# Layer norm of the first tiles in fewer VectorE steps, the transposes of the gradient half ahead of those of the next filter, and an empty slot more

## The chip, the cores and the metric

The kernel runs on one NeuronCore of a Trainium2 chip. The metric is the device time of one execution in microseconds (us), as a median over several executions. The profile is of one further execution.

The engines are named as the profile names them: PE is TensorE (matmuls; PEld its weight loads), DVE is VectorE, ACT is ScalarE, POOL is GpSimd, and SP is the queue that issues most DMAs. L938 means line 938 of the kernel before.

## The reference

Forward and backward pass of a layer that adds two branches to its input. Cut to what matters:

```python
xn = layernorm(q)                                  # [2048, 1024], eps 1e-5, steps rounded to bf16
# branch A: long convolution over the sequence, by FFT in the reference
kv  = shift(k, shift_k) * v                        # 4 taps
y   = irfft(rfft(kv) * rfft(ssm_k)) + kv * ssm_D   # one filter per channel
A   = xn * y
# branch B: gated MLP, 1024 -> 3584 -> 1024
gate, up = xn @ W_gate, xn @ W_up
h = relu(gate) * up
out = q + A + h @ W_down
# and, for a given grad_out, the gradients of q, k, v, shift_k, ssm_k, ssm_D, W_gate, W_up, W_down
```

Inputs and outputs are bf16, sums in PSUM are f32.

## The kernel before

The program is one stream for each engine. Branch B's matmuls are the bulk of the work. Branch A's are threaded between them.

**Phases of branch B.** `hidden` makes the layer norm and, in 14 blocks (seven column blocks of 512 for each half of the 16 row tiles), the matmuls of the gate (`ps_g`), of up (`ps_u`) and of the hidden gradient (`ps_h`), eight matmuls of 128x512 to a group. `grad_down` (`ps_d`) and `grad_in` (`ps_w`) make the weight gradients. `out_phase` (`ps_o`) and `grad_x` (`ps_x`) make the output and the input's gradient; nothing of branch A runs beside these two.

**The head.** The 16 row tiles are normed in chunks: four single tiles, then pairs (`LN_CHUNKS`). `layer_norm` is a generator; each `next` runs it to its next `yield`. For a chunk it does:

- the row sums on ScalarE (L866), for tile 0 with half of the columns on VectorE (L877);
- the mean in bf16 (L882 or L884), a cast of it to f32 (L891) and the subtraction (L895), all on VectorE;
- the squares, again on ScalarE (L866), with half of the columns on VectorE (L870) for tiles 0 and 1;
- the variance (L882 or L884), plus epsilon (L906), and the square root on ScalarE (L907);
- a Newton step for the root: reciprocal (L909), two products and sums (L912, L913), the reciprocal of the result (L914);
- the scaling (L920) and the store of the normed tile (L921, POOL's queue).

`flip_xn` then transposes the tile on the PE (L970, `pst_x`) and copies it to SBUF (L973). The gate of that tile waits for the copy. `first_gate_up` runs gate and up of tiles 0 to 3, with the transposes of the next tile in the middle of an up group. Before all of this `warm(17)` issues 17 dummy matmuls (L985), which depend on nothing but a memset. VectorE also makes relu(gate) * up for each up group: L1044 takes `ps_u` out of PSUM, L1046 makes `ht`. For each gradient group ScalarE copies `ps_h` (L1144) and VectorE multiplies (L1145).

**Order on the engines.** Most instructions carry a priority, and a scheduler orders those of an engine by it. `keep_in_program_order` and `pin` fix single instructions where the program issues them. Every engine then runs its own stream strictly in order: an instruction that waits holds everything queued behind it.

**Branch A.** `steps` and `slots` write it as a list of slots. Each slot holds at most one PE part and one VectorE part. It handles eight groups of 128 channels one after another. `first` begins the first group; `slots` does the rest of a group and the beginning of the next. Every slot has a nominal length (`SLOT` 1900 ns; in the dense phases `DENSE`, 1900 or 1250 ns), and every group of branch B's matmuls has one too. A slot is emitted when the nominal lengths of branch B have caught up with those of the slots so far. So a slot more moves all that follows by about one group of eight matmuls of branch B.

The transforms are matmuls with small tables (line 72: `FW`, `R`, `IA`, `RB`). Their PSUM tiles, two buffers, are copied by ScalarE (L76). Between two stages VectorE transposes 32x32 blocks (L327, two instructions of 128x1024 for a transpose, in `flip`). Of these the change touches:

- `flip_H`: the spectrum of the next group's filter, from `Bh` (after `add_D`, two small additions); read by `fwd2` about 60 us later;
- `flip_C(self.Cg, 0)`, called `flg`: the gradient half, from `Cg`, which `inv_a` and ScalarE write; read by `inv_b`, whose result `gkv` gives `gks`, which `tap_sums` (`ps<-kp,gks`) reads;
- `flip_B(self.Bk, 1)`, called `flK`: the last of a group's beginning; read by `fwd2_pair`.

**Queues.** SP issues the loads and most stores in program order: rows of x (`ln_x`), weight blocks (`wg`, `wu`, and `wdT` and `goT` by DMA transposes), and branch A's loads and stores. In the last block of `grad_down`, the normed rows come back as `xn_nat` (L961), and between them lie branch A's stores of y (`y_d`) and of the filter's gradient (`ghn`). When branch A is done, `open_right` loads `W_down` (`wd`, L1360) for `out_phase`.

Of the kernel before, what the change touches and what calls it, by code (L numbers as in the profile page):

```python
# [14 lines left out]
ALU = mybir.AluOpType  # L15
ACT = mybir.ActivationFunctionType
# [32 lines left out]
class ABranch:  # L49
# [36 lines left out]
    def load(self, out, in_):  # L86
        self.pri.now()
        ins = self.nc.sync.dma_start(out=out, in_=in_)
        if self.pin:
            self.tc.keep_in_program_order(ins)  # L90
        else:
            self.pri.pin(ins)
# [533 lines left out]
    def slots(self, st, gi):  # L626
        G, K, H, GKV = self.G, self.K, self.H, self.GKV
        if gi == 0:
            yield from self.first(st)
        nx, n2 = self.ahead(st, 1), self.ahead(st, 2)  # L630
        last = nx is None
        f2 = self.fwd2_pair()
        yield f2, None
        yield None, None
        yield f2, None
        yield None, None
        yield f2, None
        yield None, lambda: self.turn(G, 0, -1, slice(0, 4))
        q = self.cmul(H, G, True, GKV, 0)
        yield f2, q  # L640
        yield None, q
        yield None, q
        yield None, q
        yield None, q
        yield None, lambda: self.turn(G, 0, -1, slice(4, 8))
        iaG = self.inv_a()
        q = self.cmul(H, G, True, GKV, 1)
        yield None, q
        yield iaG, q
        yield None, q  # L650
        f1h = None
        if not last:
            self.need(self.load_filter, nx)
            self.need(self.load_rest, nx)
            f1h = self.fwd1_filter(nx)
        yield f1h, q
        yield None, q
        yield f1h, lambda: self.turn(H, 1, 1)
        self.fetch(n2, self.load_filter)
        q = self.cmul(K, G, True, G, 0)  # L660
        yield None, q
        yield iaG, q
        yield None, q
        if not last:
            self.need(self.load_g, nx)
            flH = self.flip_H()
            yield None, self.both(lambda: self.add_D(nx), flH)
            yield None, flH
        flg = self.flip_C(self.Cg, 0)
        yield None, flg  # L670
        yield None, flg
        yield None, q
        yield None, q
        q = self.cmul(H, K, False, K, 0)
        yield self.inv_b(st, "gkv", 0), q
        yield None, q
        yield None, q
        gkv = st["gkv"]
        gks = st["gks"] = self.ttile("gks")
        yield None, lambda: self.tt(gks[:, 0:16, :], gkv[:, 0:16, :], st["vt"][:], ALU.mult)  # L680
        self.fetch(nx, self.load_v)
        gv = self.ttile("gv")
        yield None, lambda: self.tt(gv[:, 0:16, :], gkv[:, 0:16, :], st["ksh"][:], ALU.mult)
        self.store_time(self.out_gv, st["cg"], gv)
        yield None, q
        yield None, self.both(lambda: self.halo(st), q)
        yield lambda: self.tap_sums(st), None
        self.fetch(nx, self.load_k, self.load_taps)
        f1g = None
        if not last:  # L690
            self.need(self.load_xn, nx)
            yield None, lambda: self.gate_grad(nx)
            self.fetch(n2, self.load_xn)
            f1g = self.fwd1(self.Bg, nx["gt"])
        yield None, lambda: self.tap_diagonals(st)
        ia = self.inv_a_pair()
        q = self.cmul(K, G, True, G, 1)
        yield ia, q
        yield None, q
        yield ia, q  # L700
        yield None, q
        yield None, q
        q = self.cmul(H, K, False, K, 1)
        yield f1g, q
        yield None, q
        yield f1g, q
        self.fetch(n2, self.load_g)
        yield None, q
        yield None, q
        gk = self.ttile("gk")  # L710
        tg = self.taps(st, gk, gks, [(0, 0), (1, 1), (2, 2), (3, 3)])
        yield None, tg
        yield None, tg
        yield ia, tg
        yield None, tg
        yield ia, tg
        yield None, tg
        f2H = None if last else self.fwd2(H, 1)
        yield f2H, tg
        self.store_time(self.out_gk, st["cg"], gk)  # L720
        fly = self.flip_C(self.Cy, 0)
        yield None, fly
        yield f2H, fly
        tk = None
        if not last:
            self.need(self.load_k, nx)
            self.need(self.load_taps, nx)
            self.begin(nx)
            tk = nx["tk"]
        yield None, tk  # L730
        yield None, tk
        flh = self.flip_C(self.Ch, 1)
        yield self.inv_b(st, "yt", 0), flh
        yield None, flh
        self.store_time(self.y_d, st["cg"], st["yt"])
        yield None, tk
        yield None, tk
        yield self.inv_b_chan(st, 1), tk
        yield None, tk
        yield None, tk  # L740
        if last:
            yield None, lambda: self.store_gh(st)
            return
        self.need(self.load_v, nx)
        yield None, lambda: self.start_kvt(nx)
        f1k = self.fwd1(self.Bk, nx["kvt"])
        yield None, lambda: self.store_gh(st)
        flG = self.flip_B(self.Bg, 0)
        yield f1k, None
        yield None, flG  # L750
        yield f1k, flG
        yield None, None
        flK = self.flip_B(self.Bk, 1)
        yield None, flK
        yield None, flK
        yield None, None

    def small_outputs(self):
# [20 lines left out]
class LnMlp:  # L779
# [66 lines left out]
    def layer_norm(self, xn_d, jpool, jtag, spool):  # L846

        nc, D, V = self.nc, self.D, self.nc.vector

        st0 = 0  # L850
        for i, n in enumerate(self.LN_CHUNKS):
            xt = self.ln_x[i]
            self.pri.now()
            sm = spool.tile([P, 12, 4], F32, name="ln_s")
            smb = spool.tile([P, 4, 4], BF16, name="ln_b")
            f = lambda i: sm[:, i, 0:n]
            b = lambda i: smb[:, i, 0:n]

            def half(k):
                return D // 2 if i == 0 or i == 1 and k == 2 else D  # L860
# [19 lines left out]
            def average(k, out):  # L880
                if half(k) < D:
                    return V.tensor_scalar(out=out, in0=f(k), scalar1=sm[:, k + 6, 0:1], scalar2=1.0 / D, op0=ALU.add,  # L882
                                           op1=ALU.mult)
                return V.tensor_scalar(out=out, in0=f(k), scalar1=1.0 / D, scalar2=None, op0=ALU.mult)  # L884

            for j in range(n):
                total = row_sums(j, 0, ACT.Copy)
                if i >= 1 and j == 0:
                    self.tc.keep_in_program_order(total)
            average(0, b(0))  # L890
            V.tensor_copy(out=f(1), in_=b(0))  # L891
            if i == 4:
                yield
            for j in range(n):
                centred = V.tensor_scalar(out=xt[:, j, :], in0=xt[:, j, :], scalar1=sm[:, 1, j:j + 1], scalar2=None,  # L895
                                          op0=ALU.subtract)
                if i == 4:
                    self.tc.keep_in_program_order(centred)
                if i == 1:
                    yield  # L900
                row_sums(j, 2, ACT.Square)
# [2 lines left out]
            if i == 2:  # L904
                self.tc.keep_in_program_order(var)
            V.tensor_scalar(out=b(2), in0=b(1), scalar1=LN_EPS, scalar2=None, op0=ALU.add)  # L906
            self.ln_act = nc.scalar.activation(out=f(4), in_=b(2), func=ACT.Sqrt)  # L907
            yield
            root = V.reciprocal(out=f(6), in_=f(4))  # L909
            if i == 1:  # L910
                self.tc.keep_in_program_order(root)
            V.scalar_tensor_tensor(out=f(5), in0=b(2), scalar=0.5, in1=f(6), op0=ALU.mult, op1=ALU.mult)  # L912
            V.scalar_tensor_tensor(out=b(3), in0=f(4), scalar=0.5, in1=f(5), op0=ALU.mult, op1=ALU.add)  # L913
            self.ln_dve = V.reciprocal(out=self.rstd[:, st0:st0 + n], in_=b(3))  # L914
            self.pri.now()
            for j in range(n):
# [72 lines left out]
    def hidden(self, first, goT, load, ln, tables, Wg, Wu, Wd, g, xn_d, h_d, ug_d):  # L989


        nc, HS, N = self.nc, self.ST // 2, 2 * self.FB
# [3 lines left out]
        for n in range(N):  # L996
# [7 lines left out]
            wg, wu, wdt = w  # L1004
# [165 lines left out]
                        next(ln)  # L1170

            if ahead:
                self.warm(17)
                for _ in range(3):
                    next(ln)
                next(ln)
                flip(1)
                for _ in range(4):
                    next(ln)
                yield from first_gate_up(0)  # L1180
                yield from first_gate_up(2)
# [318 lines left out]
def kernel(  # L1500
# [37 lines left out]
    b = LnMlp(tc, pri, S, D, F)  # L1538
# [9 lines left out]
    load(1)  # L1548
    first = [b.col_block(B_W_gate, 0, "wg", 0)]
    load(2)  # L1550
    load(3)
    first.append(b.col_block(B_W_up, 0, "wu", 1))
    load(4)
    first.append(b.row_block_T(B_W_down, 0, "wdT", 2))
    goT = [b.load_T(g, i, "goT", 8 + i) for i in range(2)]
# [56 lines left out]
```

## Time and profile before

| | |
|---|---|
| median of 4 runs | 1882.92 us (1882.27 to 1884.54) |
| profiled execution, its own time | 1882.52 us |
| profiled execution, first to last instruction (span) | 1880.7 us |
| TensorE busy | 1873.4 us |
| VectorE busy | 1052.1 us |
| ScalarE busy | 610.2 us |
| POOL busy | 14.9 us |
| granted TensorE clock, mean | 1.000 |
| first gate matmul | 8.94 us |
| branch A, first and last matmul | 110.96 us to about 1217 us |
| `out_phase` begins | 1297.04 us |
| `grad_x` begins | 1484.45 us |

The times of the lower rows are from the start of the span. The profile's lines read: start and duration in us, engine, line, operation, what is written and what is read, shapes, how many, and in brackets how long the engine was idle before and what ended that. Matmuls overlap, and their ends are modelled, so the distance from the start of one to the start of the next tells more than their durations.

### The profile page before, as it was taken

Reading aid. Unit: us, or ns where it says so; the run is one execution under the profiler, and the core shown is the slowest. Engines: PE = TensorE matmul, PEld = TensorE weight load, DVE = VectorE, ACT = ScalarE, POOL = GpSimd, SP = SyncE. Lnnn points to the kernel's source line nnn. Section 1 sums busy time; section 2 is a strip of 40 time slices with the busy share of each in tenths; the row PEclk is TensorE's granted clock in tenths of the full one; section 3 lists DMA queues with packets and bytes.
Section 4 is the critical chain, followed back from the end, with each engine's and each line's share of the span. In section 5 each row is a group of like instructions: output and inputs, shape, how many; then the busy total and the mean of one; then the engine's idle time right before and its main releaser. Section 6 shows DMA issues by size and latency. Waiting matters only on the chain.

```text
span 1880.7 us, 32785 instructions
## 1 busy us (share of the span) xinstructions
PE 1873.4 (100%) x13712; PEld 852.7 (45%) x13712; DVE 1052.1 (56%) x1542; ACT 610.2 (32%) x850; POOL 14.9 (1%) x37
## 2 busy tenths in 40 slices
PE   9999999999999999999999999999999999999999
PEld 4444444444444444444444444444444544444444
DVE  6676887888788685675775857500222222222222
ACT  5654354434534445444355343311000000000000
POOL 1000000000000000000000000000000000000000
PEclk9999999999999999999999999999999999999999
DMA  9897689697577665376654453495999955555553
GB/s 256 246 233 172 144 201 227 180 214 176 143 175 210 216 153 175 91 193 191 151 149 135 120 158 93 149 295 120 257 240 244 243 122 124 123 123 123 124 123 73
DMA packets 695509, 323.72 MB, mean 172 GB/s; under 512 B 524864, under 2 KB 664896, under 8 KB 695360
## 3 DMA queue, kind: packets, MB, share of 16 engines
q1 hardware_dynamic: 684864, 300.78, 64.9%
q10 hardware_dynamic: 9216, 16.65, 2.9%
q0 software_dynamic: 1280, 4.20, 0.7%
q8 instruction: 107, 1.75, 0.4%
q14 instruction: 42, 0.34, 0.1%
HBM read 143.79 MB, written 95.44 MB: 127 GB/s over the span
## 4 chain that ended last, share of the span: by engine, by line
PE 66%; DMA 0%; DVE 0%; SPq 0%; issue 0%
PE ps_x L1468 21%; PE ps_w L1237 20%; PE ps_o L1399 10%; PE ps_d L1237 9%; PE ps L72 3%; PE ps_d L1250 1%; PE ps_h L938 0%; PE ps_u L938 0%; PE ps_r L1429 0%; DMA xn_nat<-xn_d 0%; PE ps_w L1250 0%; PE ps_g L938 0%; SPq L961 0%; DVE arena L327 0%; DVE rest L1433 0%
## 5 line engine op out<-in xcount | busy, mean ns | idle before, releaser
L1237 PE MATMUL ps_w<-ugs,xn_nat 128*128 128x512 bf16 x1728 | 383.2, 379 | 0.0
L76 ACT CAST arena<-ps 128x1024 bf16<-128x1024 f32 x288 | 277.6, 1017 | 177.6 <-PE ps L72 174.0
L938 PEld LDWEIGHTS <-xnT 128*128 128x128 bf16 x1792 | 170.5, 98 | 209.2 <-issue 8.7
L1237 PEld LDWEIGHTS <-xn_nat 128*128 128x128 bf16 x1728 | 164.4, 98 | 201.2 <-issue 9.9
L327 DVE STREAM_TRANSPOSE arena<-arena 128x1024 f32<-128x1024 f32 x96 | 179.9, 1934 | 88.5 <-ACT arena L76 86.0
L938 PE MATMUL ps_u<-wu,xnT 128*128 128x512 bf16 x896 | 206.8, 379 | 0.0
L938 PE MATMUL ps_g<-wg,xnT 128*128 128x512 bf16 x896 | 204.9, 379 | 0.7 <-ACT xnT L973 0.4
L938 PE MATMUL ps_h<-wdT,goT 128*128 128x512 bf16 x896 | 205.4, 379 | 0.0
L1486 ACT ACTIVATE w<-xn,m 128x512 f32<-128x512 bf16 x32 | 24.3, 806 | 553.0 <-issue 317.2
L1468 PE MATMUL ps_x<-wgT,ggT 128*128 128x512 bf16 x896 | 198.6, 379 | 0.0
L1468 PE MATMUL ps_x<-wuT,guT 128*128 128x512 bf16 x896 | 198.6, 379 | 0.0
L1399 PE MATMUL ps_o<-wd,hT 128*128 128x512 bf16 (+1 forms) x896 | 187.6, 372 | 0.0
L1237 PE MATMUL ps_d<-g_nat,hs 128*128 128x512 bf16 x768 | 171.6, 379 | 0.0
L1468 PEld LDWEIGHTS <-guT 128*128 128x128 bf16 x896 | 87.7, 98 | 105.7
L1468 PEld LDWEIGHTS <-ggT 128*128 128x128 bf16 x896 | 87.7, 98 | 105.5
L1399 PEld LDWEIGHTS <-hT 128*128 128x128 bf16 x896 | 87.7, 98 | 99.9
L938 PEld LDWEIGHTS <-goT 128*128 128x128 bf16 x896 | 85.5, 98 | 104.6 <-issue 4.7
L1470 DVE CUSTOM_DVE_ANT_0 gx<-ps_x,gy 128x512 f32<-128x512 f32 x32 | 22.2, 692 | 185.7 <-PE ps_x L1468 185.7
L1144 ACT CAST gh<-ps_h 128x512 bf16<-128x512 f32 x112 | 65.7, 587 | 184.0 <-PE ps_h L938 177.0
L1391 DVE TENSOR_TENSOR ya<-ya,xe 128x1024 bf16<-128x1024 bf16 x16 | 11.1, 692 | 202.0 <-DMA xe<-xn_d 202.0
L1044 DVE SCALAR_TENSOR_TENSOR ru<-ru,ps_u 128x512 bf16<-128x512 bf16 x112 | 76.6, 684 | 76.4 <-PE ps_u L938 54.7
L80 DVE TENSOR_TENSOR t<-arena 128x2048 bf16<-128x2048 bf16 x96 | 114.0, 1219 | 0.4
(144 smaller groups left out, 1325.5 us busy)
## 6 DMA issues: line engine op xcount, KB each, us to landing
ug_d<-ru SPq DMA_DIRECT2D x112, 256.0 KB
ugs<-ug_d SPq DMA_DIRECT2D x112, 256.0 KB
wg<-in_B_W_gate_dram SPq DMA_DIRECT2D x56, 256.0 KB
wu<-in_B_W_up_dram SPq DMA_DIRECT2D x56, 256.0 KB
h_d<-ht SPq DMA_DIRECT2D x112, 128.0 KB
hs<-h_d SPq DMA_DIRECT2D x56, 256.0 KB
out_dram<-wi SPq DMA_DIRECT2D x56, 256.0 KB
gt<-in_grad_out_dram SPq DMA_DIRECT2D x32, 256.0 KB
```

The costliest lines, as they stand in the source:

```text
L72: self.pri.pin(self.nc.tensor.matmul(out, lhsT=lhsT, rhs=rhs, start=start, stop=stop))
L76: self.pri.pin(self.nc.scalar.copy(out=out, in_=in_))
L80: self.pri.pin(self.nc.vector.tensor_tensor(out=out, in0=in0, in1=in1, op=op))
L327: self.pri.pin(self.nc.vector.transpose(out=df[:, c0:c0 + 32, :], in_=sf[:, c0:c0 + 32, :]))
L938: self.pri.pin(self.nc.tensor.matmul(ps[:], lhsT=xT[:, kt * P:(kt + 1) * P], rhs=w(kt), start=(kt == 0), stop=(kt == self.DT - 1)), always ...
L1044: self.pri.pin(nc.vector.scalar_tensor_tensor(out=ru[s][:, 1, :], in0=ru[s][:, 0, :], scalar=0.0, in1=ps[:], op0=ALU.is_gt, op1=ALU.mult))
L1144: self.pri.pin(nc.scalar.copy(out=gh[:], in_=ps[:]))
L1237: self.pri.pin(self.nc.tensor.matmul(ps[:], lhsT=lhsT(st), rhs=rhs(st), start=(st == 0), stop=(st == self.ST - 1)))
L1399: nc.tensor.matmul(ps, lhsT=hT[:, kt, :], rhs=self.wd[:, kt, oc], start=(kt == 0), stop=(kt == self.FT - 1))
L1468: nc.tensor.matmul(ps, lhsT=T[:, kt, :], rhs=W[:, kt, oc], start=(i == 0), stop=(i == n - 1))
L1470: V.tensor_tensor_reduce(out=gx[:, oc], in0=ps, in1=gy[:, oc], scale=1.0, scalar=0.0, op0=ALU.add, op1=ALU.add, accum_out=m[:, ob:ob + 1])
L1486: nc.scalar.activation(out=w[:, oc], in_=xn[:, oc], func=ACT.Identity, scale=m[:, 7:8], bias=m[:, 6:7])
```

## The change

- In `layer_norm` the subtraction takes the bf16 mean as its scalar, and the cast to f32 is gone. The square root is taken of a quarter of the variance, which gives half the root; a new VectorE step makes a quarter of the variance; for a single tile one instruction then makes half the root plus quarter times reciprocal, where two stood; for a pair it stays at two, as plain products and sums of two tensors.
- For the first pair (i == 4) the mean is made after the `yield`, and is kept in program order.
- `warm` issues 15 dummy matmuls in place of 17.
- The load of row tile 3 stands behind the four loads of the first block of `W_up` on SP.
- In `slots`, `flg` stands ahead of `add_D` and `flip_H`.
- At the end of `slots` there is one more slot without PE and VectorE parts. It stands there once for each of the seven groups that have a next one.

```diff
@@ slots
         yield iaG, q
         yield None, q
+        flg = self.flip_C(self.Cg, 0)
+        yield None, flg
+        yield None, flg
         if not last:
             self.need(self.load_g, nx)
             flH = self.flip_H()
             yield None, self.both(lambda: self.add_D(nx), flH)
             yield None, flH
-        flg = self.flip_C(self.Cg, 0)
-        yield None, flg
-        yield None, flg
         yield None, q
         yield None, q
...
         yield None, flK
         yield None, flK
         yield None, None
+        yield None, None
@@ layer_norm
-            average(0, b(0))
-            V.tensor_copy(out=f(1), in_=b(0))
             if i == 4:
                 yield
+            mean = average(0, b(0))
+            if i == 4:
+                self.tc.keep_in_program_order(mean)
             for j in range(n):
-                centred = V.tensor_scalar(out=xt[:, j, :], in0=xt[:, j, :], scalar1=sm[:, 1, j:j + 1], scalar2=None,
+                centred = V.tensor_scalar(out=xt[:, j, :], in0=xt[:, j, :], scalar1=smb[:, 0, j:j + 1], scalar2=None,
                                           op0=ALU.subtract)
...
             V.tensor_scalar(out=b(2), in0=b(1), scalar1=LN_EPS, scalar2=None, op0=ALU.add)
-            self.ln_act = nc.scalar.activation(out=f(4), in_=b(2), func=ACT.Sqrt)
+            self.ln_act = nc.scalar.activation(out=f(4), in_=b(2), func=ACT.Sqrt, scale=0.25)
+            quarter = V.tensor_scalar(out=f(5), in0=b(2), scalar1=0.25, scalar2=None, op0=ALU.mult)
+            if i == 2:
+                self.tc.keep_in_program_order(quarter)
             yield
             root = V.reciprocal(out=f(6), in_=f(4))
             if i == 1:
                 self.tc.keep_in_program_order(root)
-            V.scalar_tensor_tensor(out=f(5), in0=b(2), scalar=0.5, in1=f(6), op0=ALU.mult, op1=ALU.mult)
-            V.scalar_tensor_tensor(out=b(3), in0=f(4), scalar=0.5, in1=f(5), op0=ALU.mult, op1=ALU.add)
+            if n == 1:
+                V.scalar_tensor_tensor(out=b(3), in0=f(6), scalar=f(5), in1=f(4), op0=ALU.mult, op1=ALU.add)
+            else:
+                V.tensor_tensor(out=f(5), in0=f(5), in1=f(6), op=ALU.mult)
+                V.tensor_tensor(out=b(3), in0=f(4), in1=f(5), op=ALU.add)
             self.ln_dve = V.reciprocal(out=self.rstd[:, st0:st0 + n], in_=b(3))
@@ hidden
-                self.warm(17)
+                self.warm(15)
@@ the loads at the start
     load(2)
+    first.append(b.col_block(B_W_up, 0, "wu", 1))
     load(3)
-    first.append(b.col_block(B_W_up, 0, "wu", 1))
     load(4)
```

## The prediction

> **What bounds the kernel now.** I read three views in this order: the page (who is busy), the waits of the PE (what stops it), and the timeline at each of those waits (how much each costs).
>
> The first line of the page settles what counts: TensorE is busy for all but 7 us, and every other engine has room.
>
> ```profile
> PE 1873.4 (100%) x13712; PEld 852.7 (45%) x13712; DVE 1052.1 (56%) x1542; ACT 610.2 (32%) x850; POOL 14.9 (1%) x37
> ```
>
> So a change gains only what it takes out of the PE's own gaps. The waits of the PE name them:
>
> ```profile
> PE ps L72 <- DVE arena L327: 0.9, 2, 0.5
> PE pst_x L970 <- DVE ln_b L884: 0.4, 2, 0.2
> PE ps_g L938 <- ACT xnT L973: 0.4, 1, 0.4
> PE ps_g L938 <- DVE xnT L973: 0.3, 1, 0.3
> PE ps_w L1250 <- DMA xn_nat<-xn_d: 0.2, 1, 0.2
> PE pst_x L970 <- DVE ln_x L920: 0.2, 1, 0.2
> ```
>
> The column is total us, times, longest. These totals are too small, because a matmul's end is modelled: it lasts 0.379 us in the records, but the next 512-wide one starts 0.216 us after it. I therefore count every start-to-start step of the PE's matmuls above 0.216 as a stall. Counted so, the first 23 us lose: 0.58 before the first gate, 0.36, 0.40 and 0.40 before the transposes of tiles 1, 2 and 3, and 0.45 before the gate of tile 3. The convolution branch (line 72) loses 4.2 us in all against the shortest group of its kind, and one load of xn_nat 0.41 at 876.
>
> VectorE's timeline, for the chain of tile 0 and for the place at 21 us (columns: start, us, what):
>
> ```profile
> 4.47 0.15 DVE L891 CAST ln_s<-ln_b 128x1 f32<-128x1 bf16 x1
> 4.66 0.48 DVE L895 TENSOR_SCALAR ln_x<-ln_x,ln_s 128x1024 bf16<-128x1024 bf16 x1
> ...
> 6.86 0.16 DVE L912 SCALAR_TENSOR_TENSOR ln_s<-ln_b,ln_s 128x1 f32<-128x1 bf16 x1
> 7.06 0.16 DVE L913 SCALAR_TENSOR_TENSOR ln_b<-ln_s 128x1 bf16<-128x1 f32 x1
> 7.25 0.16 DVE L914 RECIPROCAL rstd<-ln_b 128x1 f32<-128x1 bf16 x1
> 7.45 0.61 DVE L920 TENSOR_SCALAR ln_x<-ln_x,rstd 128x512 bf16<-128x512 bf16 x2
> ...
> 21.45 0.17 DVE L884 TENSOR_SCALAR ln_b<-ln_s 128x2 bf16<-128x2 f32 x1 [0.80 <-ACT ln_j L866]
> 21.65 0.17 DVE L891 CAST ln_s<-ln_b 128x2 f32<-128x2 bf16 x1
> 21.73 0.68 DVE L973 COPY xnT<-pst_x 128x1024 bf16<-128x1024 bf16 x1
> ```
>
> A 128x1 step costs its place in line, 0.19 to 0.20, not its 0.16. L920 at 7.45 lets the PE's transposes start at 7.86. At 21 us the copy L973, which the gate at 22.47 needs, stands behind a mean that waits for ScalarE.
>
> The branch's two worst places, in the timeline at 216 and in the chain that ended last at 628:
>
> ```profile
> 214.46 1.89 DVE L327 STREAM_TRANSPOSE arena<-arena 128x1024 f32<-128x1024 f32 x1
> ...
> 216.40 0.62 PE L72 MATMUL ps<-arena,RB 64*32 64x512 bf16 x14 [0.46 <-DVE arena L327]
> ```
>
> ```profile
> 625.94 1.84 DVE arena L327
> 627.82 0.63 PE ps L72 x32
> ```
>
> Each time the matmuls start when the second of two transposes ends.
>
> **The layer norm, walked.** Per tile the cast L891 goes (0.19), and of L912 and L913 one goes (0.20). The new multiply by 0.25 stands before the reciprocal, in the 0.23 in which VectorE waits for ScalarE's square root (6.43 to 6.66), so it is free for tile 0. The pairs of tiles keep two steps there, but their chain ends under ps_h matmuls. The subtract now takes a bf16 scalar. The trace has only f32 ones, at 0.48: below, nothing faster; above, the 128x1024 bf16 tensor_tensor (L1391), 0.69. I take 0.48, the row of the same operation; the Trainium skill ("DVE: scalar operands, raw-bit mode, write accounting and state across instructions", § 1) says that a bf16 scale costs what an fp32 one does.
>
> Now the tiles, in the order in which the changed program queues them on VectorE, each step by its distance to the next in the trace.
> - Tile 0: L920 0.38 earlier, 7.07; transposes 7.48 instead of 7.86.
> - Tile 1: 0.38 from tile 0 and 0.34 of its own (ScalarE's half of the squares, at 9.28, now ends last): L920 at 10.63 instead of 11.35, with 0.54 to the transposes as before. The PE comes there at 7.48 + 1.08 + 2.60 = 11.16 (transposes to gate, then gate and half the up, as before). Both meet: transposes at 11.17 instead of 11.89, gain 0.72; the 0.36 wait is gone.
> - Tile 2: here the order turns worse. The variance is queued ahead of the ReLU product L1044 (0.61 to the next start) and the epsilon step behind it; before, L1044 ran while ScalarE squared. The mean comes at 11.10, the subtract at 11.28, ScalarE's square (0.58 later, 1.15 long) ends at 13.01, variance 13.09, L1044 13.22, epsilon 13.83, L1046 in the square root's shadow, quarter 14.34, reciprocal 14.54, then 0.20 each: L920 at 15.14, transposes 0.53 later at 15.67 instead of 16.29. Gain 0.62.
> - Tile 3: L1044 and L1046 both stand in the chain after epsilon: subtract 15.72, square done 17.45, variance 17.53, epsilon 17.74, L1044 17.90, quarter 18.51, reciprocal 18.71, L1046 18.88, the sum 19.22, reciprocal 19.42, L920 19.62; transposes at 20.16 instead of 20.70. Gain 0.54.
> - The copy for tile 3's gate now stands ahead of the pair's mean. It starts 0.66 after its transposes (as for tile 2), not 1.03: gate at 21.57 instead of 22.47. Gain 0.90.
>
> From there to 58 us no PE step was late; the pair's L920 ends at 27.65 and its transposes are due at 27.62, so the 0.90 holds within 0.1. If a small step were free, the copy alone would give 0.36; with VectorE's order as before, about 1.2. I take 0.90.
>
> **Loads.** On SP, the load of tile 3 moves behind the four of wu, each 0.45 to 0.50 of issue; at the 350 GB/s of that stretch 1 MB more ahead of it is 3.0 us: it lands at about 12.0 by the packet records (9.0 before), and ScalarE wants it at 14.13. wu lands 0.75 sooner (first piece 9.0), wanted at 10.29. The next four are issued as before. Cost nothing; without that cover, tile 3 would be late by the difference.
>
> **Two warm-up matmuls fewer.** Row first, from the PE's weight loads, one for each dummy:
>
> ```profile
> 6.57 0.15 PEld L985 LDWEIGHTS <-warm 128*128 128x128 bf16 x1 [0.28 <-issue]
> 6.93 0.53 PEld L985 LDWEIGHTS <-warm 128*128 128x128 bf16 x3 [0.21 <-issue]
> ```
>
> The dummies start every 0.427 us until 6.57; the last three come close together, 0.216 apart: the clock opened about 5.4 us after the first. Fifteen end at 7.36, before 7.48: free. The rule speaks against it: the skill ("TensorE: Matmul & The Clock Gate", Part 1) has a free-running window of about 3.4 us that must be busy throughout, so the clock opens between 4.9 and 8.3. Seventeen slow dummies last to 8.73, fifteen to 7.87: in 0.4 of 3.4, 13% of phases, it could stay shut a window more, 1.7 us of half speed, 0.2 on average. By the row the sum has 0, by the rule 0.2. I take the row and keep 1.7 for the range.
>
> **The transposes of Cg first.** Two transposes (1.8 to 1.95 each) and add_D leave the queue ahead of inv_b. In PE groups of eight matmuls (1.73 us) between the last MLP step queued ahead of the second transpose and inv_b, the three early channel groups go from 3, 3, 5 to 5, 6, 7. inv_b stalled 0.84 at 216 and 0.23 at 373 against the shortest of its kind: 1.07 gained. What is late next: the filter's transposes, wanted 60 us later. Where VectorE runs ahead (from channel group 3), Cg is not there when its turn comes: at 665.4 VectorE would idle to 669.4, when ScalarE ends the copies, and the filter's two shift gks from 680.3 to about 684.0, its end to 685.2. The tap sums want it at 687.2. Covered by 2.0 us.
>
> **The empty slot.** It stands at the end of `slots`, so seven times, between the transposes of Bk and fwd2_pair. The first transforms after 627 had 2 groups and now have 5: 0.5 gained. The other boundaries have 3 or more. But the slots also move every later branch group by 1 to 6 MLP groups, which re-deals how often two of them stand one MLP group apart, where two PSUM buffers and ScalarE's 1.94 us of copies cost 0.21 to 0.38: nine such pairs before, 2.4 us; eleven after, 2.75. Loss 0.4. The SP queue changes too: the two ghn stores (512 KB) fall behind the last eight xn_nat loads, in a stretch with the DMA at 0.9 to 1.0: 1.3 us less ahead of the load that cost 0.41. Bounds 0 and 0.41; I take 0.3, since y_d moves closer. The wd loads come up to 7 us later and land by about 1275, wanted at 1297.
>
> **Sum.** 0.90 + 1.07 + 0.5 + 0.3 - 0.4 = 2.4 us. Against the profiled execution (1882.5, of which 1880.7 is span) 1880.1; that execution is 0.4 below the median 1882.9, so 1880.5. This is 0.13%, under the 0.2% that a measurement of this kernel can tell from no change.
>
> **Rivals.**
> - *VectorE's idle before Cg turns into tap-sum stalls (slower).* Place: channel groups 3 to 6, where flg waits for ScalarE. The point is 2.0 us of margin on gks; if VectorE falls 4 us behind that, four groups lose up to 2 us each, 8 in all, less 2.4: about 1888. For it: the 4.1 idle is certain. Against: VectorE had 1.1 idle before gks and 2.0 after. Chance 0.11.
> - *The gain is given back by new small stalls.* L1044 falls later in the queue; at 371 us a PSUM buffer of the MLP came free only 0.9 us before the PE wanted it, and a transpose is 1.9. Once or twice 1 us: 1882.2. Chance 0.16. The clock staying shut gives the same time, 0.05; a subtract at 0.69 takes 0.2 a tile, 1881.2, chance 0.04.
> - *More goes than I count.* If the pairs fall well and all of the head's waits close: 4.2 us, 1878.7. Chance 0.10.
> - The forecast, 1879.3 to 1881.9: 0.54.
>
> The range 1878.4 to 1884.0 leaves out the slow rival and the edge of the fast one. Faster by over 0.2% needs 3.8 us, 0.12; slower by it 0.11; the rest 0.77.
>
> **What would show it.** Right: no cast in the head; transposes of tile 0 near 7.48 and the gate of tile 3 near 21.6; no wait on L327 at 216 or near 630; nothing on xn_nat. Wrong: a PE wait at the tap sums after 680, dummies still at 0.427 at the end, or a subtract over 0.5.

## The result, and the profile after

The changed kernel takes 1880.49 us (median of 42 runs), the kernel before 1882.58 (60 runs): a ratio of 0.9988, 95% interval 0.9984 to 0.9993, so 2.1 us or 0.11% faster. The forecast was 1880.5. The profiled execution's span is 1878.7 instead of 1880.7. The total came out as worked out; several of its terms did not, and they cancelled. That it hit to a hundredth is luck, the more so as the kernel before came out 0.34 lower here than the 1882.92 from which the forecast was counted. What follows takes the terms one by one.

The first line of the page and the waits of the PE after (columns of the waits: total us, times, longest us):

```profile
PE 1872.1 (100%) x13710; PEld 852.1 (45%) x13710; DVE 1050.6 (56%) x1538; ACT 609.8 (32%) x850; POOL 14.8 (1%) x37
```

```profile
PE pst_x L978 <- DVE ln_x L928: 0.8, 1, 0.8
PE ps_g L946 <- ACT xnT L981: 0.4, 1, 0.4
PE ps_g L946 <- DMA wg<-in_B_W_gate_dram: 0.4, 1, 0.4
PE ps_u L946 <- DMA wu<-in_B_W_up_dram: 0.2, 1, 0.2
```

The branch's wait on the transposes (L327), both waits on small layer norm steps, the wait of the fourth gate on VectorE's copy and the one on xn_nat are gone. The wait on L928 stands only behind the warm-up matmuls and costs nothing by itself. Two lines are new, and neither was in the forecast: a load of gate weights and a load of up weights for which the PE stops.

Counted as before, in start-to-start steps of the PE's matmuls above their usual 0.216, the difference of the two traces (one execution each) is this:

| place | gain forecast, us | gain in the traces, us |
|---|---|---|
| head, to the gate of tile 3 | 0.90 | 1.51 (22.47 to 20.96) |
| from there to 60 us: goT at 26, wg at 55 | 0 | -0.65 (0.13 + 0.52) |
| inverse transform at 215 and 373 | 1.07 | 1.07 |
| first transforms at 627 | 0.5 | 0.5 |
| wu at 237 | 0 | -0.39 |
| xn_nat (near 870) | 0.3 | 0.36 |
| branch groups one MLP group apart | -0.4 | -0.4 (nine, with a small stall at 187 that is none of them, 2.49; eleven, 2.89) |
| sum | 2.4 | 2.0 |

**The head.** The PE's timeline after has the transposes (L978) and the gate of tile 3:

```profile
7.55 0.66 PE L978 MATMUL pst_x<-ident,ln_x 128*128 128x128 bf16 x8 [0.79 <-DVE ln_x L928]
...
11.26 0.62 PE L978 MATMUL pst_x<-ident,ln_x 128*128 128x128 bf16 x8
...
15.44 0.62 PE L978 MATMUL pst_x<-ident,ln_x 128*128 128x128 bf16 x8
...
19.55 0.62 PE L978 MATMUL pst_x<-ident,ln_x 128*128 128x128 bf16 x8
...
20.96 1.90 PE L946 MATMUL ps_g<-wg,xnT 128*128 128x512 bf16 x8
```

Forecast were 7.48, 11.17, 15.67, 20.16 and 21.57. Tiles 0 and 1 are within 0.1, tile 2 is 0.23 ahead of the forecast and tile 3 0.61. VectorE's timeline for tile 3 shows why:

```profile
17.44 0.16 DVE L908 TENSOR_SCALAR ln_b<-ln_b 128x1 bf16<-128x1 bf16 x1
17.51 0.68 DVE L1052 SCALAR_TENSOR_TENSOR ru<-ru,ps_u 128x512 bf16<-128x512 bf16 x1
18.11 0.15 DVE L910 TENSOR_SCALAR ln_s<-ln_b 128x1 f32<-128x1 bf16 x1
18.17 0.15 DVE L914 RECIPROCAL ln_s<-ln_s 128x1 f32<-128x1 f32 x1
18.24 0.41 DVE L1054 TENSOR_TENSOR ht<-ru 128x512 bf16<-128x512 bf16 x1
18.57 0.21 DVE L918 SCALAR_TENSOR_TENSOR ln_b<-ln_s 128x1 bf16<-128x1 f32 x1
18.81 0.16 DVE L922 RECIPROCAL rstd<-ln_b 128x1 f32<-128x1 bf16 x1
19.01 0.48 DVE L928 TENSOR_SCALAR ln_x<-ln_x,rstd 128x1024 bf16<-128x1024 bf16 x1
```

Start minus start is what a step costs. L908 (epsilon), L910 (quarter) and L914 (reciprocal) cost 0.06 to 0.07 each, though each lasts 0.15: the step that follows each of them does not read it. L918 and L922 cost 0.24 and 0.20: what follows reads them. The walk charged 0.16 to 0.20 to every one. (In tile 0 the last steps are chained, and there L918, whose scalar is a tile and no constant, takes 0.25 to the next start instead of 0.20; hence 7.55 for 7.48.)

The head's gain is not that of one pair of executions: the gate of tile 3 starts at 20.82 to 21.14 in the seven traces with the new head and its loads, and at 22.47 to 22.96 in the four with the old head.

The copy that the gate at 20.96 needs no longer stands behind a mean, as forecast:

```profile
20.21 0.69 DVE L981 COPY xnT<-pst_x 128x1024 bf16<-128x1024 bf16 x1 [0.71 <-PE pst_x L978]
20.82 0.16 DVE L885 TENSOR_SCALAR ln_b<-ln_s 128x2 bf16<-128x2 f32 x1
```

And the subtract with the bf16 scalar costs what the f32 one did, 0.49 against 0.48, as the nearest row had it and as the Trainium skill ("DVE: scalar operands, raw-bit mode, write accounting and state across instructions", § 1) says; the bound of 0.69 is out.

**The transposes of Cg first.** At 215 the second transpose of Cg (L327 at 208.27, VectorE's timeline) now ends 4.3 us ahead of the inverse transform, which follows its MLP group without a wait:

```profile
208.27 1.95 DVE L327 STREAM_TRANSPOSE arena<-arena 128x1024 f32<-128x1024 f32 x1
...
214.56 0.62 PE L72 MATMUL ps<-arena,RB 64*32 64x512 bf16 x16
```

**The slow rival.** VectorE does idle for Cg once it runs ahead, 6.5 us before 670.58, more than the 4.1 forecast:

```profile
670.58 3.71 DVE L327 STREAM_TRANSPOSE arena<-arena 128x1024 f32<-128x1024 f32 x2 [6.51 <-ACT arena L76]
...
684.28 1.22 DVE L80 TENSOR_TENSOR gks<-gkv,vt 128x2048 bf16<-128x2048 bf16 x1
```

gks starts at 684.28 (forecast 684.0), and the tap sums that read it start at 690.03 without a wait. The margin is over 4 us there, and the PE has no wait at all that the view lists from 640 to 1300.

### The profile page after: what moved, and what is told of

Read it like the earlier page. It is cut to its first block, busy times and chain, and to the rows that moved or that the text cites. A ratio compares the mean times of both kernels' runs of the same rounds, so it can differ in the third digit from the quotient of the medians.

```text
span 1878.7 us, 32768 instructions
## 1 busy us (share of the span) xinstructions
PE 1872.1 (100%) x13710; PEld 852.1 (45%) x13710; DVE 1050.6 (56%) x1538; ACT 609.8 (32%) x850; POOL 14.8 (1%) x37
## 4 chain that ended last, share of the span: by engine, by line
PE 99%; DMA 1%; DVE 0%; issue 0%; SPq 0%; ACT 0%; DVEq 0%
PE ps_x L1476 21%; PE ps_w L1245 20%; PE ps_u L946 10%; PE ps_h L946 10%; PE ps_g L946 10%; PE ps_o L1407 10%; PE ps_d L1245 9%; PE ps L72 5%; PE ps_d L1258 1%; PE ps_w L1258 1%; PE ps_r L1437 0%; DMA wg<-in_B_W_gate_dram 0%; DMA wu<-in_B_W_up_dram 0%; PE pst_x L978 0%; DMA ln_x<-in_A_q_dram 0%
## 5 line engine op out<-in xcount | busy, mean ns | idle before, releaser
L327 DVE STREAM_TRANSPOSE arena<-arena 128x1024 f32<-128x1024 f32 x96 | 180.4, 1934 | 118.2 <-ACT arena L76 116.7
```

The costliest lines, as they stand in the source:

```text
L327: self.pri.pin(self.nc.vector.transpose(out=df[:, c0:c0 + 32, :], in_=sf[:, c0:c0 + 32, :]))
```

## The experiments

The traces of all experiments lack some matmul records (about 1 in 60). Steps there were counted over the program's order, so that a gap in the records is no stall. "Lead" is how much earlier than in the kernel before (58.90) the shift rows' first product starts, right after the first gate of block 1: it sums all that happened to the PE until then.

### One edit at a time

The three parts of the diff, each alone on the kernel before: the head (layer norm, its order, warm-up, loads), the transposes, the slot.

> The kernel before with the whole head of the change (layer norm steps, mean's place in the queue, 15 warm-up matmuls, load of tile 3 behind wu) and neither of the other two edits. Theory (the head gains 1.51 us, and the loads of the next stage, which do not come earlier, take part of it back): gate of tile 3 at 20.96 instead of 22.47, a wait on goT of about 0.13 near 26 and one on the gate weights of block 1 of about 0.5 near 55, so the lead left at 60 us is about 0.85; the convolution branch as before (0.84 at 215 and 0.23 at 373 on the inverse transform, 0.5 at 627, nine pairs, 2.4 us), xn_nat 0.4. Time 0.9 us below before. Rival: the wait at 55 belongs to the flip order or the empty slot; then it is absent here, the lead at 60 us is 1.4 to 1.5, and the time is 1.5 below before.

> The kernel before with only the transposes of Cg ahead of the filter's. Theory: the inverse transform's stalls at 215 (0.84) and 373 (0.23) fall under 0.06, PE order is that of before so the nine pairs stay (2.36 us), as do 0.5 at 627 and 0.41 on xn_nat; no PE wait at the tap sums; time 1.07 below before. Rival on record (VectorE's idle before Cg comes back as stalls at the tap sums of channel groups 3 to 6, up to 2 us each): 6 to 8 us slower. Second rival: the wait of 0.39 on wu at 237 comes from this edit; then it is seen here and the gain is 0.7.

> The kernel before with only the empty slot more. Theory: the 0.5 at 627 and the 0.41 on xn_nat go, the pairs one MLP group apart become eleven to twelve (2.9 us instead of 2.4), the inverse transform keeps 0.84 at 215 and 0.23 at 373, and wu of the block at 237 is late by 0.2 to 0.4, because the slot moves branch loads in SP's queue: net 0.0 to 0.4 below before, not to be told from it. Rival: the wu wait comes from the earlier head or from the transposes' order; then it is absent and the gain is 0.4 to 0.8.

Measured, each against the kernel before at 1882.57: the head alone 1881.22 (0.9994, 0.9988 to 1.0001), the transposes alone 1882.04 (0.9998, 0.9989 to 1.0006), the slot alone 1882.41 (0.9997, 0.9989 to 1.0006). None of the three can be told from no change by its time. The gains of the medians, 1.35 + 0.53 + 0.16 = 2.04, add up to what the whole change has, but each is known only to within 1.2 to 1.6 us either way, so the agreement proves little. The traces say more:

- *Head alone.* Gate of tile 3 at 21.13, then 0.94 of waits on wg near 55, so the lead was 0.41 here, not 0.85. The inverse transform, 627 and the pairs are as before; xn_nat costs 0.21. The rival (the wg wait comes from another edit) is out.
- *Transposes alone.* The inverse transform's stalls at 215 and 373 are gone. But wu of block 5 costs 0.37 near 239, and that of the next block 0.19 at 286. So these waits belong to this edit; the third prediction, which put them on the slot, was wrong. xn_nat costs 0.85. No wait at the tap sums: the slow rival is out here too.
- *Slot alone.* 627 is clean, and xn_nat falls to 0.04, so both are the slot's doing. The 0.36 for xn_nat is the loosest number of the table, though: with the slots and spacing of before it cost 0.41, 0.21 and 0.85 in three traces, and with the slot 0.04 in all six that have the old spacing. wu at 237 is on time. The pairs cost what they cost in the changed kernel; the inverse transform keeps 0.83 at 215 and loses 0.41 instead of 0.23 at 374.

Why does winning 0.84 at 215 make wu late at 237? The table by stretch, 205 to 232 us, in the trace with the transposes alone (columns: stretch, its length, then busy us and instructions of PE, PEld, DVE, ACT, POOL; clock; DMA share; GB/s):

```profile
205.00:232.00 27.00, 26.84 (x195) 12.34 (x197) 25.91 (x35) 7.24 (x11) 0.40 (x1) 1.00 0.52 136
```

VectorE is busy for 25.9 of 27 us, and its timeline has no idle from 205.7 to 232. The PE won time there, VectorE could not. SP's timeline of the changed kernel shows what hangs on that:

```profile
227.55 1.36 SPq L96 DMA_DIRECT2D out_dram<-gv  x2
228.95 1.14 SPq L1058 DMA_DIRECT2D h_d<-ht  x1
230.19 3.06 SPq L939 DMA_DIRECT2D wu<-in_B_W_up_dram  x4
```

The stores of gv and h wait for VectorE's products, and the loads of wu stand behind them in the same queue. In the kernel before, wu was issued 2.2 us ahead of the block's first gate (231.4, 233.6), here 1.6 (230.2, 231.8):

```profile
231.37 3.03 SPq L931 DMA_DIRECT2D wu<-in_B_W_up_dram  x4
```

To try this, the loads were put ahead of the store:

```
-                yield from run(up, sp + 3)
+                up(sp + 3)
                 load_up()
+                yield from step(self.PACE[1])
```

> The changed kernel with the loads of the next block's up weights issued ahead of the store that belongs to the last up product of a block, in all blocks but the first. Theory (wu is late at 237 because SP holds its load behind a store of h that waits for VectorE, and VectorE has no idle time from 206 to 232, so the 0.84 that the PE won at 216 does not reach it): the first piece is issued about 1.1 earlier relative to the block's first gate, the waits of 0.39 at 237 fall under 0.1, time 0.3 to 0.4 below the changed kernel. Rival A: the loads wait for the PE to free the buffers anyway; nothing moves. Rival B: the store held back keeps a tile of ht from VectorE and the PE waits for it elsewhere, same time or slower.

Measured: 1880.23 (0.9987, 0.9981 to 0.9994), 0.26 under the changed kernel, which the times cannot tell. In the trace:

```profile
225.86 3.44 SPq L939 DMA_DIRECT2D wu<-in_B_W_up_dram  x4
229.41 1.36 SPq L96 DMA_DIRECT2D out_dram<-gv  x2
230.83 2.29 SPq L1058 DMA_DIRECT2D h_d<-ht  x1
```

wu is issued 7.0 us before the block's first gate (232.8) and lands in time: the wait at 237 is gone, and there is none on wu after 61 us. (Block 1's wu, which this edit does not move, is late by 0.55 at 60.5 in this trace.) It moved further than expected because it passes the stores of gv as well. That the PE was merely later here is not the reason: in the trace with all cures (e9_all, below) it comes to this place earlier than in the changed kernel, and there is no wait either. The cause is shown; its size is the trace's 0.39.

### What eats the head's gain: the wg load at 55

First the loads' order, which the prediction had costed at nothing.

```
-    first.append(b.col_block(B_W_up, 0, "wu", 1))
     load(3)
+    first.append(b.col_block(B_W_up, 0, "wu", 1))
```

> The changed kernel with the load of tile 3 back ahead of the four wu loads. Theory (the swap does nothing for the head, and the late gate weights at 55 come from the earlier start of the stage): gate of tile 3 within 0.1 of 20.96, waits at 26 and 55 as in the changed kernel (0.13 and 0.52), time within 0.3 of it. Rival A: wu lands 0.75 later and is late for the up of tile 0 (wanted at 10.36), a wait of 0.2 to 0.7 near 10.4 and the head's gain smaller by that. Rival B: the swap is what makes the later loads late; then the waits at 26 and 55 go, and the kernel is 0.5 faster than the changed one.

Measured: 1881.11 (0.9990, 0.9984 to 0.9997). In its trace wu of tile 0 is late, by 0.33, 0.46 and 0.15 in the steps up to 13.2; the PE's timeline names the load:

```profile
10.84 0.60 PE L946 MATMUL ps_u<-wu,xnT 128*128 128x512 bf16 x2 [0.17 <-DMA wu<-in_B_W_up_dram]
11.74 0.59 PE L946 MATMUL ps_u<-wu,xnT 128*128 128x512 bf16 x2 [0.30 <-DMA wu<-in_B_W_up_dram]
```

The gate of tile 3 is at 21.67, 0.71 later than in the changed kernel, and wg costs 1.30 near 55, so that the lead is -0.54: nothing of the head is left. Rival A holds: with the head earlier, the up of tile 0 needs the swap. The traces of the transposes and of the slot alone, which have the old loads and the old head, also lose 0.78 and 0.17 at the up of tile 0, which the kernel before did not show in its one profiled execution. So even the old head can lose at this place. Its time alone, 0.6 above the changed kernel, does not settle the size.

Then the wg load itself. The PE's step at which it waits, and SP's timeline of the changed kernel ahead of it:

```profile
55.79 2.32 PE L946 MATMUL ps_g<-wg,xnT 128*128 128x512 bf16 x10 [0.36 <-DMA wg<-in_B_W_gate_dram]
```

```profile
37.71 6.86 SPq L957 DMA_TRANSPOSE wdT<-in_B_W_down_dram  x3
...
45.28 1.37 SPq L957 DMA_TRANSPOSE wdT<-in_B_W_down_dram  x1
...
49.14 2.21 SPq L939 DMA_DIRECT2D wg<-in_B_W_gate_dram  x4
```

Block 1's W_down, wanted only after 60 us, is issued ahead of its gate weights; its four transposing loads hold SP for 8.2 us, where the four plain ones of wg take 2.2. In the kernel before, SP issued wg 0.64 earlier than this, though its PE was the later one:

```profile
48.50 2.19 SPq L931 DMA_DIRECT2D wg<-in_B_W_gate_dram  x4
```

Half of block 1's W_down was moved behind wg and wu:

```
                         if sp in (0, 4):
                             load(6 + sp // 4)
-                        if sp == 0:
-                            for q in range(4):
-                                load_down(q)
+                            for q in range(2):
+                                load_down(sp // 2 + q)
```

> The changed kernel with two of block 1's four W_down pieces issued after the gate and up weights of that block instead of ahead of them. Theory (the gate weights at 55 are late because of what stands ahead of them in the DMA, not because of their own issue): 512 KB less ahead of them is 1.5 us at 350 GB/s, the last gate piece lands near 54.3 instead of 55.8, the wait at 55 (0.52) is gone, and at 60 us the PE is 1.4 to 1.5 ahead of the kernel before instead of 0.86; time 0.5 below the changed kernel. Rival A: the landing hangs on when the buffers come free (issue at 49.1), then it stays at 55.5 or later and the wait too. Rival B: the moved pieces are late for the first gradient product of block 1 near 62 and the PE waits there for 0.5 or more.

Measured: 1879.67 (0.9984, 0.9977 to 0.9990), 0.8 under the changed kernel. SP after the edit:

```profile
36.32 5.18 SPq L957 DMA_TRANSPOSE wdT<-in_B_W_down_dram  x2
...
45.76 2.16 SPq L939 DMA_DIRECT2D wg<-in_B_W_gate_dram  x4
```

No wait at 26 or 55, and a lead of 1.54: the head's 1.51 arrives whole. But the reason expected was not quite right. I had counted 1.5 us of bytes in the DMA; wg moved 3.4 us, because it is issued 3.4 us sooner, and its last piece lands 5.3 after its issue as against 4.9. Over nine traces with the old order that lag is 4.8 to 5.6 too. What is late is SP's turn, not the transfer; why transposing loads hold SP so long was not tried. With the new head and the old W_down order, leads were 0.41, 0.86, 0.81, 0.39 and 0.28 in five traces, with the last wg piece landing between 55.8 and 56.3 whatever the head did. The times lie closer together as well: the 21 runs with half of W_down moved between 1879.32 and 1880.13, the 42 of the changed kernel between 1879.46 and 1883.26. That fits a wait whose length changes from run to run, but was not followed further.

### Small steps on VectorE, by themselves

Four series of eight 128x1 f32 steps were put on VectorE in the forward output stage, where it idles (written short; k runs from 0 to 7):

```
+ t[:, 0] = t[:, 0] * 0.5                       each reads the one before
+ t[:, 8 + k] = t[:, 24] * 0.5                  none reads another
+ t[:, 1] = t[:, 2] * 0.5 + t[:, 1]             immediate scalar, chained
+ t[:, 1] = t[:, 2] * t[:, 1] + t[:, 3]         scalar from the step before
```

> The changed kernel with four series of eight 128x1 f32 steps added on VectorE in the forward output stage, where VectorE is mostly idle: tensor_scalar in place (each reads the one before), tensor_scalar into eight other columns (none reads another), scalar_tensor_tensor in place with an immediate scalar, and the same with its scalar read from the step before. Theory (the head came out 0.6 better than walked because steps that do not read the one before start 0.06 to 0.07 after it): distances 0.19 to 0.20, 0.06 to 0.07, 0.20 and 0.25. Rival: every small step holds its place for 0.15 to 0.20 whether dependent or not, and the head's surplus has another source; then the second series has 0.15 or more. Time within 0.3 of the changed kernel.

Measured: 1880.22. VectorE's timeline at the series:

```profile
1355.29 1.46 DVE L1406 TENSOR_SCALAR probe<-probe 128x1 f32<-128x1 f32 x8
1356.66 0.57 DVE L1408 TENSOR_SCALAR probe<-probe 128x1 f32<-128x1 f32 x8
1357.15 1.50 DVE L1410 SCALAR_TENSOR_TENSOR probe<-probe 128x1 f32<-128x1 f32 x8
1358.69 2.00 DVE L1413 SCALAR_TENSOR_TENSOR probe<-probe 128x1 f32<-128x1 f32 x8
```

The distances in each series are 0.188, 0.060, 0.194 and 0.255. A step's own record is nearly the same in the first two (0.153 and 0.144). So the recorded duration of these steps says nothing about their cost; whether the next one reads the result does. A scalar that is read from the step before costs 0.06 more than an immediate one.

### The pairs, and all cures together

In the changed kernel fourteen branch groups stand one MLP group behind another in PE order, and eleven of them lose 0.21 to 0.30. One such pair, from the timelines of the PE and of ScalarE:

```profile
704.58 0.42 PE L72 MATMUL ps<-gt,R 32*64 32x512 bf16 x8
704.94 1.90 PE L1245 MATMUL ps_d<-g_nat,hs 128*128 128x512 bf16 x8
706.77 0.66 PE L72 MATMUL ps<-gt,R 32*64 32x512 bf16 x8
```

```profile
705.04 1.93 ACT L76 CAST arena<-ps 128x1024 bf16<-128x1024 f32 x2 [1.49 <-PE ps L72]
```

Between the two stand only eight MLP matmuls, and the second takes 0.66 for what the first does in 0.42. Of its eight matmuls four start at 706.77 and four at 707.02, just after ScalarE has emptied the second of the first group's two PSUM buffers at 706.97. In the last two MLP stages the branch's steps with and without PE work are spaced 1900 and 1250 ns, 3150 for one of each: 1.8 groups of 1730, so sometimes one and sometimes two. With 2300 and 1120 the sum is 3420, 1.98 groups:

```
-    SLOT, DENSE = 1900, (1900, 1250)
+    SLOT, DENSE = 1900, (2300, 1120)
```

> The changed kernel with the branch's steps in the last two MLP stages spaced 2300 and 1120 instead of 1900 and 1250 (with and without PE work), which leaves 4 instead of 14 places in PE order where two branch groups stand one MLP group apart. Theory (each such pair costs 0.21 to 0.30 because two PSUM buffers wait for ScalarE's copies): of the eleven stalls, 2.89 us in all, those after 640 go but for one or two; pairs cost 0.7 to 1.0, time 1.9 below the changed kernel, 1878.6. Rival: steps without PE work come closer, 1120 apart, and VectorE falls behind: stalls of 1 us or more at the transposes and tap sums after 640, time the same or slower.

Measured: 1878.25 (0.9977, 0.9967 to 0.9986), 2.2 under the changed kernel. Two such stalls are left, 0.24 at 264.8 and 0.28 at 769.9, and VectorE keeps up. The slot had only re-dealt the pairs; the spacing removes them.

> The changed kernel with the three cures together: two W_down pieces behind the gate and up weights in the first block, the up loads ahead of the last store of h, branch steps 2300 and 1120 apart in the last two stages. Theory (the three losses are separate): 0.8 + 0.3 + 2.2 below the changed kernel, 1877.2, with no wait on wg at 55, none on wu after 230 and two pair stalls left (0.5). Rival: the cures share a cause or stand in each other's way on SP's queue; then 1878.0 or more.

> The kernel before with the same three cures and none of the change. Theory (the change itself wins 1.54 in the head, 1.07 at 215 and 373, 0.5 at 627 and 0.4 on xn_nat, of which the two kernels shown kept only 2.0 because of the wg and wu waits and the pairs): the pairs fall from 2.4 to about 0.6, the rest of the ledger stays, time about 1880.8, so 3.4 to 3.7 above the changed kernel with the cures. Rival: the change is worth the same 2.0 with the cures as without; then 1879.2.

Measured: the changed kernel with the three cures 1877.46 (0.9972, 0.9960 to 0.9983), the kernel before with them 1880.51 (0.9988, 0.9982 to 0.9995). The first beats both kernels shown. The waits on wg at 55 and on wu at 237 are gone; what is left is 0.13 on goT at 26, 0.25 at 62 where a piece of the W_down that was moved back lands at 62.6 (a price of that edit), two pairs (0.52), and 0.09 on xn_nat. The change is worth 3.05 us between these two, and 2.1 without the cures: nearer to the ledger's 3.4 to 3.7 than to the rival's 2.0. Of what it is short, the traces show two parts: with the spacing xn_nat costs nothing in the kernel before either, and the wait of 0.25 at 62 is in the changed kernel alone.

## Why the prediction was right

- *Tile 0 and 1, one step less each, the subtract at the same price: right*, within 0.1.
- *"then 0.20 each" in the walk of tiles 2 and 3: the term that was mis-sized.* Its ground, "a 128x1 step costs its place in line, 0.19 to 0.20", had been read from chained steps alone. Steps that the next one does not read cost 0.06; the head gained 1.51 instead of 0.90.
- *"The 0.90 holds within 0.1" to 58 us: wrong.* The step looked at VectorE's pair only and not at SP's queue, where the last piece of wg landed at 55.1 for a use at 56.65. A PE that came 1.5 us earlier, to a wg issued 0.64 later, ran into it: with the 0.13 on goT, 0.65 in the changed kernel, 0.75 to 1.3 in the four others with its head and its loads.
- *"Loads. Cost nothing": wrong in sign.* Undoing the swap made wu late by 0.94, and the gate of tile 3 by 0.71.
- *Warm-up: nothing against it.* All eight traces with fifteen dummies have the fast steps by the end (below); no run has this edit alone.
- *The transposes first: right in its gain*, 1.07, and right that the tap sums keep their margin. Missing was that VectorE has no idle behind 216, so that SP's loads did not move with the PE; 0.39 came back at 237. "L1044 falls later in the queue" was named among the small stalls, but the mechanism was the store ahead of wu on SP.
- *Slot: right.* 0.5 at 627, 0.36 on xn_nat, 0.4 lost to pairs.

So the total was right by luck, through two errors of opposite sign: 0.61 too little in the head, and 1.04 too little given back, next to 0.06 more on xn_nat. The path (which waits go, and in what order the tiles follow) was right; the loads behind the head were not looked at.

## What to carry to other kernels

A stall that is taken away gains only until the next resource that did not move: ask of each DMA behind it when it is issued, what stands ahead of it in its queue, and by which engine that is paced. Order loads in a queue by when they are wanted, not by when their buffers come free. In a chain of small VectorE steps, count the ones that the next step reads. And a schedule that puts two streams together by their mean spacing meets its bad phase again and again; choose the spacing so that it rarely does (here two stalls were left of eleven).

## What was not expected of the hardware

The clock of TensorE opened at another time in each execution, though all begin with the same dummies (fifteen or seventeen): these turned from 0.427 to 0.216 us a step 2.5 to 5.8 us after the first, over twelve traces (2.53, 3.32, 3.38, 3.39, 3.81, 4.16, 4.18, 4.24, 4.59, 5.44, 5.46, 5.83; each is good to about 0.3). The granted clock of the profile reads 1.00 in these us too, so the turn can be read from the steps alone. The earliest and a late one, the weight loads of the trace with the slot alone, and of that with wu ahead of the store:

```profile
3.58 0.15 PEld L986 LDWEIGHTS <-warm 128*128 128x128 bf16 x1 [0.28 <-issue]
4.01 2.12 PEld L986 LDWEIGHTS <-warm 128*128 128x128 bf16 x10 [0.28 <-issue]
```

```profile
6.57 0.15 PEld L993 LDWEIGHTS <-warm 128*128 128x128 bf16 x1 [0.28 <-issue]
6.92 0.10 PEld L993 LDWEIGHTS <-warm 128*128 128x128 bf16 x1 [0.20 <-issue]
```

Every sequence, of fifteen dummies or of seventeen, had the clock open by its end, though in the second of these traces only two of fifteen were fast. The Trainium skill's free-running window ("TensorE: Matmul & The Clock Gate", Part 1) does fit a time that varies from run to run; a window of 3.4 us that has to be busy from end to end does not fit 2.53. The 0.2 on average that the rule asked for is not seen, but at a chance of 13% the eight traces with fifteen dummies are too few to exclude it.
